# A gated linear-attention layer and an ELU feed-forward block: two engines' gating put in sequence, table loads placed by hand, and block sums moved

## The chip, the cores and the metric

The kernel runs on one core of a Trainium2 chip. The core has four compute engines that run their own instruction streams side by side and wait for one another through semaphores: TensorE (PE, matrix products), VectorE (DVE, elementwise work), ScalarE (ACT, functions by table, and copies) and GpSimd (POOL, elementwise work too). SyncE (SP) issues DMAs; GpSimd and ScalarE issue some as well. The metric is the device time of one execution in microseconds (us); lower is better. "Bank" below is a bank of PSUM, the memory that TensorE writes its sums to.

## The reference

The first block is a recurrence over 768 tokens, for 4 batches and 8 heads of 48 channels, with complex decay; only the real part is read out:

```python
mag = np.sqrt(a_re * a_re + a_im * a_im)
scale = np.minimum(mag, 0.999) / (mag + 1e-06)
a_re_n, a_im_n = (a_re * scale, a_im * scale)
for t in range(S):
    new_re = ar * S_re - ai * S_im
    new_im = ar * S_im + ai * S_re
    S_re, S_im = (new_re + kv, new_im)          # kv = outer product of k[t], v[t]
    y[:, :, t] = q[t] @ S_re
```

Its output, 3072 tokens by 384, goes through a feed-forward block: `h = x @ w_in` (384 by 2048), `g = ELU(h)`, `out = g @ w_out` (2048 by 384). All is float32.

## The kernel before

**Units.** A unit is two batches times 128 tokens; there are 12, numbered 0 to 11. Units u and u+2 hold the same batches, so state and the running angle pass from u to u+2. A unit goes through: the logarithm of the decay's magnitude and its angle (`squares`, `joined`, `logarithms`, `powers`, `lengths`, `ratios`, `slopes`, `angles`, `carried`: ACT, DVE, POOL), sums over tokens by TensorE (`decays`, `turns`), sine and cosine (`waves`, ACT), scaling of q and k by the decays (`scaled`), multiplication of q and k by sine and cosine (`gated`, line 1000), transposes (`transposed`, line 1020, copied out by ACT on line 1021), scores, states and values, and then the feed-forward layer of its 256 tokens.

**Gating.** `gated` is one multiplication of 128 by 1536 elements for k (tile `kg`) and one for q (tile `qg`). From unit 4 on, k's is done by GpSimd and q's by VectorE, issued k first. Both wait for the cosine (line 974).

**The angle's carry.** `carry_on` (line 859) sends the last token's angle of unit u by a DMA on GpSimd's queue to a row in device memory; `carry_back` (line 820) fetches that row by a second DMA on the same queue into one row of the tile `w`, once `slopes` (line 780) no longer reads it; `carried` (line 826) adds it to the angle of unit u+2, one instruction on VectorE; and `turns` (line 837, TensorE) sums the angles.

**The layer from unit 3 on.** The first product, by w_in, is done with 20 block products P0 to P19 (`mult`, line 1438, four blocks of 128 by 128 each) in place of 24. Their right-hand sides are the sums that `mixed` makes of the blocks of x (line 1406 on VectorE; line 1412, one sum, on GpSimd: it overwrites the block that the sum `pair` reads, so it waits for `pair`). Their left-hand sides are blocks of w_in and block sums of w_in (`summed_in`, lines 1394 and 1396), made once on VectorE. The 20 products add up in five banks (z, w, b, x, y) in the order `ORDER`; intermediate sums are taken out by ACT (`kept`, line 1451) and VectorE (`joint`, line 1454). A later product of the same bank therefore waits until the copy that needs the earlier sum is done: P3, the third product of bank z, waits for the copy of P8+P1 ("21"), and P12, the second of bank x, for the copy of P2 ("01"). The second product, by w_out, is done with seven (`product`, line 1316) in place of eight; its weight sums are made once by `combined` (line 1275), and its results leave by lines 1324, 1328, 1335, 1337 and 1341. The three banks b, z, w come free when these results have been read, w last of all (the third output sum of line 1337).

**ELU.** `low` (lines 1459 and 1460, ACT) makes exp(min(h,0)), `whole_of` (line 1463, VectorE) the rest. ACT holds one set of function tables at a time; where a function is not in the set that is loaded, the build puts a load (ACT_TABLE_LOAD) before the instruction.

**The order of the work** is written out by hand. Units 0 to 2 and part of unit 3 follow the list `first`, with idle products `warm` (line 1537) for TensorE between; what comes later is put at due times (`put`), in sixteenths of a unit's period, and sorted. Within one engine instructions run strictly in that order. Around the change, ACT has sine, absolute value, cosine, then the squares of the next unit, then the copies of the layer; TensorE has products of unit u's layer with the transposes of unit u+1 between; VectorE, in units 2 and 3, also makes the block sums of both weights, and from there tests weights (`test`, line 680).

Of the kernel before, what the change touches and what calls it, by code (L numbers as in the profile page):

```python
# [10 lines left out]
FP32 = mybir.dt.float32  # L11
U32 = mybir.dt.uint32
AF = mybir.ActivationFunctionType
ALU = mybir.AluOpType
PSUM = bass.MemoryType.PSUM

C = 128
# [488 lines left out]
def kernel(  # L506
# [12 lines left out]
    nc = tc.nc  # L519
# [4 lines left out]
    HD = H * D  # L524
# [161 lines left out]
    def flat(t):  # L686
        return t.rearrange("p n h d -> p (n h d)")
# [128 lines left out]

    def carry_back(u):

        if u in carry:
            nc.gpsimd.dma_start(out=flat(nat[u]["w"])[0:1], in_=carry[u])  # L820

    def carried(u):

        if u in carry:
            row = nat[u]["th"][0:1].rearrange("p n h d -> p (n h d)")
            nc.vector.scalar_tensor_tensor(
                out=row, in0=flat(nat[u]["w"])[0:1], scalar=float(2 * np.pi), in1=row, op0=ALU.mult,
                op1=ALU.add,
            )

# [24 lines left out]
    def carry_on(u):  # L855
        nxt = u + B // NB
        if nxt < NU:
            carry[nxt] = dram.tile([1, NB * HD], FP32, tag="carry", bufs=2, name="carry")
            nc.gpsimd.dma_start(out=carry[nxt], in_=flat(nat[u]["z"])[C - 1 : C])

    def turns(u):
# [126 lines left out]
            scaled(u, "k")  # L988
        nc.vector.tensor_tensor(out=x["q"], in0=x["q"], in1=x["E"], op=ALU.mult)

    def gated(u, part=None):

        x = nat[u]
        step = NB if part is None else 1
        n = part or 0
        for key in ("k", "q") if part is None else ("q", "k"):
            eng = products(u) if key == "k" else nc.vector
            each = x[key][:, n : n + step].rearrange("p n h d -> p (n h) d")
            to = gates[key][:, n : n + step].rearrange("p n h i d -> p (n h) i d")
            eng.tensor_tensor(  # L1000
                out=to[:, :, :, 0:D], in0=each.unsqueeze(2).to_broadcast([C, step * H, 2, D]),
                in1=x["cs"][:, n * H : (n + step) * H], op=ALU.mult,
            )
# [189 lines left out]
        inner(u, f)  # L1193
        elu(u, f)

    def table(name):
        nc.scalar.preload_act_table_set(name)

    def inner(u, f):
# [152 lines left out]
        "z": (8, 1, 3, 16, 17, 15), "w": (6, 5, 14, 10, 4, 11), "b": (7,), "x": (2, 12, 13),  # L1352
        "y": (9, 0, 18, 19),
    }
    ORDER = 8, 1, 7, 6, 3, 9, 5, 0, 2, 14, 12, 10, 16, 18, 4, 17, 19, 13, 11, 15
    IN_OF = {
# [41 lines left out]
    def mixed(u):  # L1398

        x = nat[u]  # L1400
        b = x["x"].rearrange("p k (n t) -> p (k n) t", n=2)
        six = new("x", 2, [C, NI, GT]).rearrange("p k (n t) -> p (k n) t", n=2)
        lo, hi = halves, pair

        def both(to, a, c, op):
            nc.vector.tensor_tensor(out=to, in0=a, in1=c, op=op)

        two = six[:, 0:1].to_broadcast([C, 2, C])
        both(six[:, 0:3], b[:, 0::2], b[:, 1::2], ALU.add)
        both(lo, b[:, 0:2], b[:, 2::3], ALU.add)  # L1410
        both(hi, two, six[:, 1:3], ALU.add)
        nc.gpsimd.tensor_tensor(out=six[:, 0], in0=b[:, 3], in1=b[:, 4], op=ALU.add)
        both(b[:, 2::3], b[:, 2:4], b[:, 4:6], ALU.subtract)
        both(six[:, 3:5], b[:, 0:2], six[:, 1:3], ALU.add)
        both(six[:, 5], lo[:, 0], lo[:, 1], ALU.add)
        x["mix"] = {
            0: hi[:, 1], 18: hi[:, 1], 15: hi[:, 0], 9: six[:, 1], 12: six[:, 1], 4: six[:, 2],
            2: six[:, 3], 10: six[:, 4], 16: six[:, 5], 5: six[:, 0], 17: lo[:, 0], 1: lo[:, 1],
            3: lo[:, 1], 19: b[:, 2], 7: b[:, 5], 6: b[:, 3], 8: b[:, 3], 11: b[:, 1],
            13: b[:, 0], 14: b[:, 4],  # L1420
        }

    def opened_banks(u):

# [124 lines left out]

    def decays_of(u, *at):  # L1550
        fns = squares, joined, logarithms, powers, lengths, ratios, slopes, noted, angles, carried
        put(at[6] + 0.3, carry_back, u)
        put(at[0], begun, u)
        for x, fn in zip(at, fns):
            put(x, fn, u)

    def gates_of(u, *at):
# [20 lines left out]
        (values, 0, 0), (powers, 1), (convert,), (states, 0, 1), (lengths, 1), (load_qk, 1),  # L1578
        (convert,), (ratios, 1), (values, 0, 1), (seam, 0), (warm, 2), (warm, 2), (decays, 1),
        (load_a, 2), (warm, 1), (inner, 0, 0), *2 * [(convert,)], (noted, 1), (scaled, 1),  # L1580
        (warm, 2), (convert,), (load_v, 1), (slopes, 1), (ends, 1), *3 * [(convert,)],
        (inner, 0, 2), (elu, 0, 0), (convert,), (fetch, "in", 4), (angles, 1), (turns, 1),
        (waves, 1), (gated, 1, 0), (inner, 0, 4), (gated, 1, 1), (transposed, 1, "q", 0),
        (transposed, 1, "k", 0), (convert,), (scores, 1, 0), (load_v, 2), (convert,),
# [13 lines left out]
        *3 * [(convert,)], (elu, 1, 12), (load_qk, 2), *4 * [(convert,)], (inner, 1, 14),  # L1598
        (elu, 1, 14), (logarithms, 2), (powers, 2), *4 * [(convert,)], (project, 1, 0, 0, 4),
        (project, 1, 1, 0, 4), *3 * [(convert,)], (noted, 2), (lengths, 2), (ratios, 2),  # L1600
        (slopes, 2), (carry_back, 2), (load_a, 3), (angles, 2), (carried, 2), (convert,), (project, 0, 1, 0, 4),
        (convert,), (project, 0, 0, 4, 8), *3 * [(convert,)], (decays, 2), (project, 1, 0, 4, 8),
        *2 * [(convert,)], (project, 1, 1, 4, 8), (turns, 2), *2 * [(convert,)],
        (project, 0, 1, 4, 8), (begun, 3), (squares, 3), *2 * [(convert,)],
# [1 line left out]
        (load_qk, 3), (logarithms, 3), (powers, 3), (project, 1, 1, 8, 12),  # L1606
        (states, 2, 0), (project, 1, 0, 12, 16), (transposed, 2, "q", 0), (lengths, 3),
        (ratios, 3), (project, 0, 0, 8, 12), (transposed, 2, "k", 0), (transposed, 2, "q", 1),
        (slopes, 3), (carry_back, 3), (angles, 3), (project, 1, 1, 12, 16), (transposed, 2, "k", 1),
        (carried, 3), (scored, 2), (turns, 3), (project, 0, 1, 8, 12), (valued, 2), (seam, 2),  # L1610
        (noted, 3), (project, 0, 0, 12, 16), (waves, 3), (scaled, 3), (ends, 3),
        (project, 0, 1, 12, 16), (opened,),
# [1 line left out]
    def layer_of(u, at_h, at_p):  # L1614
        if u == PAIRED:
            for m in range(NF // 2):
                put(at_h + m, hidden, u, 2 * m)
            put(at_h + 3, folded, u, 0, (3, 1))
            put(at_h + 7, folded, u, 1, (3, 1))
        else:  # L1620
            put(at_h, opened_banks, u)
            for n, p in enumerate(ORDER):
                put(at_h + 0.4 * n, mult, u, p)
            for at, fn, *args in (
                (1.5, kept, "21", "z"), (2.5, kept, "31", "b"),
                (3.5, joint, "31", "31", "w", ALU.add),
                (4.5, joint, "31", "31", "z", ALU.subtract), (5.6, low, "31", "31"),
                (6.6, whole_of, "31", "31"), (6.5, kept, "30", "w"),
                (7.5, joint, "20", "y", "21", ALU.subtract), (8.5, kept, "01", "x"),
                (9.5, kept, "10", "w"), (11.5, joint, "20", "20", "w", ALU.add),  # L1630
                (12.4, low, "20", "20"), (13.4, whole_of, "20", "20"),
                (12.5, joint, "30", "z", "30", ALU.subtract),
                (10.5, kept, "00", "x"),
                (13.5, joint, "00", "00", "y", ALU.add),
                (14.5, joint, "21", "21", "w", ALU.subtract), (15.4, low, "21", "21"),
                (16.45, whole_of, "21", "21"), (15.5, joint, "00", "z", "00", ALU.subtract),
                (16.4, low, "00", "00"), (17.45, whole_of, "00", "00"),
                (16.5, joint, "30", "30", "y", ALU.subtract), (17.4, low, "30", "30"),
                (18.45, whole_of, "30", "30"), (17.5, joint, "10", "x", "10", ALU.subtract),
                (18.4, low, "10", "10"), (19.55, whole_of, "10", "10"), (19.4, low, "11", "w"),  # L1640
                (20.4, whole_of, "11", "w"), (19.5, joint, "01", "01", "z", ALU.subtract),
                (20.5, low, "01", "01"), (21.5, whole_of, "01", "01"),
            ):
                put(at_h + 0.4 * at, fn, u, *args)
            put(at_h + 0.4 * 17.6, folded, u, 0, (3, 1))
            put(at_h + 0.4 * 22, folded, u, 1, (3, 1))
        ks = [(k, h) for k in (1, 4, 2, 5, 6, 7, 3) for h in range(2)]
        step = 8 / len(ks)
        for m, (k, h) in enumerate(ks):
            put(at_p + m * step, product, u, k, h)  # L1650
        for h in range(2):
            put(at_p + (2.2 + h) * step, folded, u, h, (2,))
            put(at_p + (6.2 + h) * step, folded, u, h, (4,))

    for u in range(2, NU):
# [4 lines left out]
        if u == 2:  # L1660
            decays_of(u, 16, 16, 17, 17, 18.4, 19.5, 19.6, 22.7, 19.8, 19.8)
            gates_of(u, 20.4, 21.6, 22.1, 22.4, 22.4, 22.6)
        else:
            sq = (r + 7.2, r + 9.6) if u == PAIRED + 2 else (r + 3.4, r + 5)
            decays_of(u, *sq, r + 12.8, r + 13.2, r + 13.4, r + 13.5, r + 14.9, r + 15.7, r + 15.5, r + 16.6)
            gates_of(u, r + 15, r + 18.32, r + 18.5, r + 18.6, r + 18, r + 19.7)
            if u > PAIRED + 1:
                put(r + 16.8, scaled, u, "k", None)
        if u > PAIRED:
# [5 lines left out]
            put(at, valued, u)  # L1675
            put(at, seam, u)
            put(r + 34.45, mixed, u)
        layer_of(u, r + 36, r + 44)
    for n in range(len(SUMS)):
        put(37 + 0.65 * n, summed_in, n)  # L1680
    for m, x in enumerate(((1, 0), (2, 0), (1, 1), (4, 0), (2, 1), (4, 1), (3, 0), (3, 1))):
        put(37.2 + m * 0.6, combined, *x)
    for m in range(NR):
        put(40 + 2.75 * m, test_fetch, m)
        put(42.2 + 2.75 * m, test)
# [41 lines left out]
```

## Time and profile before

| | us |
|---|---|
| median of 3 runs | 699.52 (698.95 to 702.98) |
| the profiled execution's own time | 702.24 |
| its span, first to last instruction | 700.4 |
| TensorE busy | 652.6 (93%) |
| VectorE busy | 519.8 (74%) |
| ScalarE busy | 426.6 (61%) |
| GpSimd busy | 172.9 (25%) |

A period of one unit in the steady part (units 4 to 11, from about 231 us on) takes about 53.2 us. TensorE's clock is full but for a few stretches. The views used are: the waits of TensorE (who was waited for, us in total, times, longest), the timeline (start, duration, engine, line, operation, tiles; in square brackets the idle time before it and who ended it), and a table of stretches (busy time of each engine, then the granted TensorE clock).

### The profile page before, as it was taken

What the parts mean: (1) busy time and instruction counts of PE and PEld (TensorE: products, weight loads), DVE (VectorE), ACT (ScalarE), POOL (GpSimd) and SP (SyncE); (2) the same over time, 40 slices, a digit from 0 to 9 for tenths busy, and PEclk for the clock granted to TensorE, in tenths of its full rate; (3) what the DMA queues carried; (4) which work ended last, traced back from release to release, by engine and by line L of the source; (5) the groups of instructions that cost most, each with busy time, mean ns of one, the idle gap of its engine ahead of it and who ended that gap; (6) DMA issues with size and microseconds to landing.
All of it is one profiled execution on the core that took longest, in us unless ns stands there. A gap on an engine that the chain in (4) does not pass through costs nothing.

```text
span 700.4 us, 17232 instructions
## 1 busy us (share of the span) xinstructions
PE 652.6 (93%) x7232; PEld 586.1 (84%) x7232; DVE 519.8 (74%) x790; ACT 426.6 (61%) x692; POOL 172.9 (25%) x202
## 2 busy tenths in 40 slices
PE   8899899899989899899899999999999899899995
PEld 6777686477878799899899899899899899899995
DVE  5889899763988868778678768868868858855381
ACT  6875356665726567577477477477477477372250
POOL 2000000122124404603603603703702701502000
PEclk9899999999989999999999999999999999999998
DMA  9996645330913521630652342441450560210000
GB/s 164 176 159 96 152 149 166 61 70 20 162 32 63 99 60 48 113 75 28 115 92 49 75 99 53 85 99 43 87 106 23 99 113 24 53 32 13 18 1 29
DMA packets 151507, 56.12 MB, mean 80 GB/s; under 512 B 129748, under 2 KB 143228, under 8 KB 151420
## 3 DMA queue, kind: packets, MB, share of 16 engines
q1 hardware_dynamic: 147616, 53.58, 38.0%
q0 software_dynamic: 3584, 1.21, 1.5%
q8 instruction: 59, 0.97, 0.6%
q14 instruction: 28, 0.23, 0.1%
q10 hardware_dynamic: 220, 0.14, 0.1%
HBM read 48.91 MB, written 4.81 MB: 77 GB/s over the span
## 4 chain that ended last, share of the span: by engine, by line
PE 45%; DVE 27%; ACT 19%; issue 6%; DMA 1%; ACTq 1%; POOL 0%; DVEq 0%; POOLq 0%
PE mlp L1316 16%; PE mlp L1438 6%; DVE qg L1000 5%; PE y L1438 5%; PE w L1020 4%; PE w L1061 3%; PE mlp L1207 3%; PE y L1106 3%; PE y L1133 2%; ACT L1460 1%; ACT L735 1%; ACT qt L1021 1%; DVE g L1454 1%; ACT ee L1460 1%; DVE n L842 1%
## 5 line engine op out<-in xcount | busy, mean ns | idle before, releaser
L1316 PE MATMUL mlp<-w_out,g 128*128 128x192 f32 x640 | 115.0, 331 | 3.0 <-DVE o L1337 2.8
L1316 PEld LDWEIGHTS mlp<-w_out,g 128*128 128x128 f32 x640 | 105.5, 192 | 7.1 <-DVE o L1337 5.1
L1078 POOL TENSOR_TENSOR S<-S,T 128x384 f32<-128x384 f32 x36 | 33.5, 930 | 204.4 <-DVE S L1076 204.4
L1207 PE MATMUL mlp<-x,w_in 128*128 128x256 f32 x288 | 68.2, 394 | 3.2 <-DVE g L1218 2.9
L1463 DVE SCALAR_TENSOR_TENSOR g<-ee,g 128x512 f32<-128x512 f32 x63 | 43.9, 696 | 31.9 <-ACT ee L1460 31.8
L1207 PEld LDWEIGHTS mlp<-x,w_in 128*128 128x128 f32 x288 | 55.8, 197 | 12.6 <-DVE g L1218 3.3
L1294 DVE TENSOR_TENSOR g<-g 128x512 f32<-128x512 f32 x80 | 59.2, 751 | 5.7 <-PE mlp L1316 4.6
L1438 PE MATMUL mlp<-x,w_in 128*128 128x128 f32 x432 | 58.5, 279 | 4.1 <-DVE o L1337 3.4
L1438 PEld LDWEIGHTS mlp<-x,w_in 128*128 128x128 f32 x432 | 52.4, 192 | 7.1 <-DVE o L1337 5.2
L1454 DVE TENSOR_TENSOR g<-g,mlp 128x512 f32<-128x512 f32 x45 | 30.7, 683 | 35.6 <-PE mlp L1438 34.8
L1316 PE MATMUL mlp<-w,g 128*128 128x192 f32 x320 | 54.7, 329 | 0.0
L1316 PEld LDWEIGHTS mlp<-w,g 128*128 128x128 f32 x320 | 51.8, 190 | 0.7
L1021 ACT COPY qt<-w 128x512 f32<-128x512 f32 x48 | 25.9, 589 | 43.5 <-PE w L1020 43.5
L1459 ACT ACTIVATE ee<-g 128x512 f32<-128x512 f32 x63 | 39.5, 627 | 19.3 <-DVE g L1454 18.9
L1460 ACT ACTIVATE ee<-ee 128x512 f32<-128x512 f32 x72 | 45.4, 631 | 2.1
L1187 POOL DMA_DIRECT2D x<-y x62 | 29.9, 489 | 59.6 <-ACT y L1123 37.1
L970 ACT ACTIVATE cs<-n 128x768 f32<-128x768 f32 (+1 forms) x14 | 10.5, 751 | 54.8 <-DVE n L845 54.8
L1000 DVE TENSOR_TENSOR qg<-q,cs 128x1536 f32<-128x1536 f32 (+1 forms) x12 | 40.4, 3367 | 0.0
L1020 PE MATMUL w<-ident,qg 128*128 128x128 f32 x192 | 26.6, 285 | 11.4 <-DVE qg L1000 11.2
L820 POOL DMA_DIRECT2D n<-carry x10 | 5.4, 538 | 121.9 <-DVE n L780 67.3
L1020 PEld LDWEIGHTS w<-ident,qg 128*128 128x128 f32 x192 | 22.7, 147 | 14.2 <-DVE qg L1000 13.7
L901 ACT ACTIVATE n<-w 64x384 f32<-64x384 f32 (+1 forms) x60 | 28.1, 486 | 9.3 <-PE w L886 8.7
(217 smaller groups left out, 1480.0 us busy)
## 6 DMA issues: line engine op xcount, KB each, us to landing
w<-in_moe_w_out_dram SPq DMA_DIRECT2D x8, 768.0 KB, 4.3
g<-in_moe_w_in_dram SPq DMA_DIRECT2D x24, 256.0 KB, 3.6
g<-in_moe_w_out_dram SPq DMA_DIRECT2D x24, 256.0 KB
w<-in_moe_w_in_dram SPq DMA_DIRECT2D x16, 288.0 KB, 5.4
vn<-in_v_dram SPq DMA_DIRECT2D x24, 192.0 KB, 4.2
out_dram<-o SPq DMA_DIRECT2D x48, 96.0 KB, 2.8
ar<-in_a_re_dram SPq DMA_DIRECT2D x22, 192.0 KB, 3.3
ai<-in_a_im_dram SPq DMA_DIRECT2D x22, 192.0 KB, 5.2
```

The lines of the kernel that those rows point to most:

```text
L1000: eng.tensor_tensor(out=to[:, :, :, 0:D], in0=each.unsqueeze(2).to_broadcast([C, step * H, 2, D]), in1=x["cs"][:, n * H : (n + step) * H], ...
L1020: nc.tensor.transpose(t[:, h], of, ident)
L1021: nc.scalar.copy(out=o[:, h0 : h0 + 4], in_=t)
L1078: eng.tensor_tensor(out=new_s, in0=new_s, in1=wide, op=ALU.mult)
L1207: nc.tensor.matmul(t[:, e], lhsT=w_in[:, i, ts(f + e, C)], rhs=x["x"][:, i], start=(i == 0), stop=(i == NI - 1),)
L1294: nc.vector.tensor_tensor(out=S_of(u, k, h), in0=a, in1=b, op=op)
L1316: nc.tensor.matmul(to, lhsT=a[:, m], rhs=b[:, m], start=(first and h == 0 and m == 0), stop=False, skip_group_check=True,)
L1438: nc.tensor.matmul(x["c" + c][:, ts(m, C)], lhsT=a[:, m], rhs=x["mix"][p], start=(p == BANKS[c][0] and m == 0), stop=False, skip_group_che ...
L1454: nc.vector.tensor_tensor(out=part(u, to), in0=part(u, a), in1=part(u, b), op=op)
L1459: nc.scalar.activation(out=e, in_=part(u, of), func=AF.Relu, scale=-1.0)
L1460: nc.scalar.activation(out=e, in_=e, func=AF.Exp, scale=-1.0)
L1463: nc.vector.scalar_tensor_tensor(out=part(u, to), in0=nat[u]["e", to], scalar=-1.0, in1=part(u, of), op0=ALU.add, op1=ALU.max,)
```

## The change

1. `gated` takes the tensors as an argument. For units 4 to 11, q's part (VectorE) is put at r+19.7 and k's (GpSimd) at r+19.8. Between them stands `mixed_rest`, which holds two operations taken out of `mixed`: VectorE's `pair` and GpSimd's sum that waits for it. GpSimd runs in order, so its gating of k now stands behind VectorE's gating of q. In unit 3 VectorE does q before k.
2. For units 4 to 11, one load of a table set that has arctangent and sine stands before `angles`, where two loads stood (one before the arctangent, one before the sine); and the load of the exponential's set stands behind the squares and ahead of the copies "21" and "31", where it stood between the two steps of the first `low`. That is one load fewer per unit.
3. P7 is the sixth product and not the third: 8, 1, 6, 3, 9, 7, 5, ... The sum "31" is made in another order accordingly: P6 is copied out of bank w, bank z subtracted, bank b added.
4. The block sums of w_in: the first 11 at steps of 0.6 and not 0.65, the other 10 (from 45.4 on) past unit 3's scores and states; the last two of `combined` at 46 and 47, where 40.8 and 41.4 were.
5. For units 2 and 3 the carried row stays on the chip, in a row of the tile `more`, so `carry_back` and its DMA are gone and `carried` reads that row.
6. One `warm` of 2 in the list `first` (ahead of unit 1's `ends`) is 4.

```diff
     def carry_back(u):
-        if u in carry:
+        if u in carry and u > 3:
             nc.gpsimd.dma_start(out=flat(nat[u]["w"])[0:1], in_=carry[u])
...
-                out=row, in0=flat(nat[u]["w"])[0:1], scalar=float(2 * np.pi), in1=row, op0=ALU.mult,
+                out=row, in0=carry[u] if u < 4 else flat(nat[u]["w"])[0:1], scalar=float(2 * np.pi), in1=row, op0=ALU.mult,
...
         if nxt < NU:
-            carry[nxt] = dram.tile([1, NB * HD], FP32, tag="carry", bufs=2, name="carry")
+            if nxt < 4:
+                carry[nxt] = more[0:1].rearrange("p a b -> p (a b)")[:, ts(nxt % 2, NB * HD)]
+            else:
+                carry[nxt] = dram.tile([1, NB * HD], FP32, tag="carry", bufs=2, name="carry")
             nc.gpsimd.dma_start(out=carry[nxt], in_=flat(nat[u]["z"])[C - 1 : C])
...
-    def gated(u, part=None):
+    def gated(u, part=None, keys=("k", "q")):
...
-        for key in ("k", "q") if part is None else ("q", "k"):
+        for key in keys if part is None else ("q", "k"):
...
-    ORDER = 8, 1, 7, 6, 3, 9, 5, 0, 2, 14, 12, 10, 16, 18, 4, 17, 19, 13, 11, 15
+    ORDER = 8, 1, 6, 3, 9, 7, 5, 0, 2, 14, 12, 10, 16, 18, 4, 17, 19, 13, 11, 15
...
-        two = six[:, 0:1].to_broadcast([C, 2, C])
         both(six[:, 0:3], b[:, 0::2], b[:, 1::2], ALU.add)
         both(lo, b[:, 0:2], b[:, 2::3], ALU.add)
-        both(hi, two, six[:, 1:3], ALU.add)
-        nc.gpsimd.tensor_tensor(out=six[:, 0], in0=b[:, 3], in1=b[:, 4], op=ALU.add)
...
+    def mixed_rest(u):
+        b = nat[u]["x"].rearrange("p k (n t) -> p (k n) t", n=2)
+        six = nat[u]["six"]
+        nc.vector.tensor_tensor(
+            out=pair, in0=six[:, 0:1].to_broadcast([C, 2, C]), in1=six[:, 1:3], op=ALU.add
+        )
+        nc.gpsimd.tensor_tensor(out=six[:, 0], in0=b[:, 3], in1=b[:, 4], op=ALU.add)
...
-        (warm, 2), (convert,), (load_v, 1), (slopes, 1), (ends, 1), *3 * [(convert,)],
+        (warm, 4), (convert,), (load_v, 1), (slopes, 1), (ends, 1), *3 * [(convert,)],
...
-                (1.5, kept, "21", "z"), (2.5, kept, "31", "b"),
-                (3.5, joint, "31", "31", "w", ALU.add),
-                (4.5, joint, "31", "31", "z", ALU.subtract), (5.6, low, "31", "31"),
-                (6.6, whole_of, "31", "31"), (6.5, kept, "30", "w"),
+                (1.5, kept, "21", "z"), (2.5, kept, "31", "w"),
+                (4.5, joint, "31", "31", "z", ALU.subtract),
+                (5.5, joint, "31", "31", "b", ALU.add), (6.6, low, "31", "31"),
+                (7.6, whole_of, "31", "31"), (6.5, kept, "30", "w"),
...
-            decays_of(u, *sq, r + 12.8, r + 13.2, r + 13.4, r + 13.5, r + 14.9, r + 15.7, r + 15.5, r + 16.6)
-            gates_of(u, r + 15, r + 18.32, r + 18.5, r + 18.6, r + 18, r + 19.7)
+            decays_of(u, *sq, r + 12.8, r + 13.2, r + 13.4, r + 13.5, r + 14.9, r + 15.7, r + 15.52, r + 16.6)
+            gates_of(u, r + 15, r + 18.32, r + 18.5, r + 18.6, r + 18)
+            put(r + 19.7, gated, u, None, ("q",))
+            put(r + 19.8, gated, u, None, ("k",))
+            if u > PAIRED + 1:
+                put(r + 19.45, table, "exp_and_others", u)
+                put(r + 15.5, table, "trig_and_small", u)
...
             put(r + 34.45, mixed, u)
+            put(r + 35.75, mixed_rest, u)
...
-        put(37 + 0.65 * n, summed_in, n)
+        put(37 + 0.6 * n if n < 11 else 45.4 + 0.6 * (n - 11), summed_in, n)
...
-        put(37.2 + m * 0.6, combined, *x)
+        put(37.2 + m * 0.6 if m < 6 else 40 + m, combined, *x)
```

More of the change, by code (lines that the diff above doesn't have):

```diff
@@ L1194, in hidden, with table @@
         elu(u, f)
-    def table(name):
+    def table(name, u=None):
         nc.scalar.preload_act_table_set(name)
@@ L1421, in mixed @@
         }
+        x["six"] = six
+    def mixed_rest(u):
[5 more added lines that the diff above has]
+        nc.gpsimd.tensor_tensor(out=six[:, 0], in0=b[:, 3], in1=b[:, 4], op=ALU.add)
     def opened_banks(u):
@@ L1551, in decays_of @@
         fns = squares, joined, logarithms, powers, lengths, ratios, slopes, noted, angles, carried
-        put(at[6] + 0.3, carry_back, u)
+        if u > 3:
+            put(at[6] + 0.3, carry_back, u)
         put(at[0], begun, u)
@@ L1600 @@
         (project, 1, 1, 0, 4), *3 * [(convert,)], (noted, 2), (lengths, 2), (ratios, 2),
-        (slopes, 2), (carry_back, 2), (load_a, 3), (angles, 2), (carried, 2), (convert,), (project, 0, 1, 0, 4),
+        (slopes, 2), (load_a, 3), (angles, 2), (carried, 2), (convert,), (project, 0, 1, 0, 4),
         (convert,), (project, 0, 0, 4, 8), *3 * [(convert,)], (decays, 2), (project, 1, 0, 4, 8),
@@ L1608 @@
         (ratios, 3), (project, 0, 0, 8, 12), (transposed, 2, "k", 0), (transposed, 2, "q", 1),
-        (slopes, 3), (carry_back, 3), (angles, 3), (project, 1, 1, 12, 16), (transposed, 2, "k", 1),
+        (slopes, 3), (angles, 3), (project, 1, 1, 12, 16), (transposed, 2, "k", 1),
         (carried, 3), (scored, 2), (turns, 3), (project, 0, 1, 8, 12), (valued, 2), (seam, 2),
```

## The prediction

> **What bounds the kernel now.** I read the waits of TensorE first, since it is busy for 93% of the span:
>
> ```profile
> PE w L1020 <- DVE qg L1000: 11.2, 8, 1.7
> PE mlp L1438 <- DVE o L1337: 3.4, 5, 1.7
> PE w L1061 <- DVE S L1076: 3.0, 3, 2.4
> PE w L837 <- DVE n L826: 2.7, 2, 1.6
> PE y L1438 <- ACT g L1451: 2.4, 8, 0.3
> ```
>
> The first and last rows come once in each of units 4 to 11; the third and fourth are single holes. The timeline of unit 7 shows the repeated one:
>
> ```profile
> 391.07 0.84 ACT L970 ACTIVATE cs<-n 128x768 f32<-128x768 f32 x1 [5.53 <-DVE n L845]
> ...
> 393.75 3.75 POOL L1000 TENSOR_TENSOR kg<-k,cs 128x1536 f32<-128x1536 f32 x1 [0.92 <-POOL x L1412]
> ...
> 394.26 0.82 ACT L710 ACTIVATE n<-ai 128x768 f32<-128x768 f32 x1
> 394.37 4.75 DVE L1000 TENSOR_TENSOR qg<-q,cs 128x1536 f32<-128x1536 f32 x1
> ...
> 394.99 1.05 ACT L1451 COPY g<-mlp 128x512 f32<-128x512 f32 x2
> ...
> 395.60 1.16 PE L1438 MATMUL mlp<-halves,g 128*128 128x128 f32 x8
> ...
> 399.17 1.09 PE L1020 MATMUL w<-ident,qg 128*128 128x128 f32 x8 [1.51 <-DVE qg L1000]
> ...
> 405.41 1.16 PE L1438 MATMUL y<-x,w_in 128*128 128x128 f32 x8 [0.30 <-ACT g L1451]
> ```
>
> q's gating takes 4.75 us beside GpSimd's; in unit 2, where VectorE does both, it takes 1.75. It ends 1.62 us after k's, so it stood still until then. P3 (395.60) starts when the copy "21" is out (394.99 to 395.52): just in time. The row at 405.41 is P12; after it TensorE runs without a hole to 430. So a unit's cost here is the time from the sine's start (391.07) to P12: 14.34 us in units 7 to 9, 14.31 or 14.32 in 5, 6, 10 and 11, 14.69 in 4.
>
> Last, the table of stretches about the hole in unit 3 (TensorE's busy time stands first, its clock third from the end):
>
> ```profile
> 200.00:202.00 2.00, 0.00 (x0) 0.00 (x0) 2.00 (x4) 0.00 (x0) 0.00 (x0) 0.98 0.03 10
> 202.00:204.00 2.00, 1.79 (x60) 1.78 (x60) 1.66 (x4) 0.00 (x0) 1.03 (x2) 0.50 0.03 8
> 206.00:208.00 2.00, 2.00 (x8) 2.00 (x7) 2.00 (x4) 0.94 (x2) 1.21 (x1) 0.50 0.00 0
> ```
>
> A hole of 2.41 us is followed by 6.6 us (202.0 to 208.6) at half clock.
>
> **Part 1, gating in sequence, with parts 2 and 3, for units 4 to 11.** They act on one stretch and are summed together, from unit 7's rows.
> VectorE: `pair` leaves the front (0.33), so the third output sum ends at 394.12 and not 394.45; q's gating runs 394.04 to 395.79, then `pair` to 396.12. Queued behind these on GpSimd: the sum of line 1412 (0.52), then k's gating 396.7 to 400.45, then line 716 and the state sums, which nobody needs before 420. Line 1454 reads one operand from PSUM and ran at its usual 0.73 beside GpSimd at 399.36, so VectorE's next work isn't held.
> ACT: the merged trigonometric load takes 1.28 us out of an idle stretch of 5.53: worth nothing; if that idle time were gone it would be worth 1.28. The exponential's load stands behind line 710 and ahead of the copies: 395.10 to 396.38, "21" to 396.93, "31" to 397.45.
> TensorE: P8, P1 from 391.60; P6 was covered by P7 and now needs bank w at once: it waits from 393.38 to 394.2 for line 1337. P3 needs "21": it waits from 395.1 to 396.97. Then nothing waits: P3, P9, P7 (3 of 0.893), q's transposes (0.873), P5, P0 (1.786), k's transposes (0.873, at 402.3; kg has been ready since 400.5), P2, P14 (1.786), and 0.1 for the restart: P12 at 405.06. ACT's copies "01" (to 404.95) are then only just in time. The sine-to-P12 time is 13.99, against 14.34.
> So of the removed wait of 1.51 nearly all comes back as P3's wait for the copy behind the load. Gain: 0.35 in units 5, 7, 8, 9, 10 (1.75), 0.7 in unit 4, 0 in unit 6 (there line 710 came a microsecond late for a DMA, which now delays P3), and 1.8 in unit 11, where no squares stand ahead of the load: 4.25 in all.
> The rule that speaks against it: the Trainium skill, "ScalarE: Activation LUTs", "What ACT_TABLE_LOAD costs", puts a switch of sets at about 2.66 us, 1.28 of load and 1.38 of drain. By that P3 would wait 1.3 us more in seven units: a loss of 5 rather than a gain of 4. But the row shows the Relu of line 1459 ending at 401.49, a load of 1.28, and the exponential starting at 402.80: 1.31 in all. I take the row.
>
> **The clock under the new holes.** TensorE now stands 0.8 us, works 0.9, and stands 1.9. The Trainium skill, "TensorE: Matmul & The Clock Gate", "HAM oscillation", asks only for no idle gap over about 3.4 us: by it nothing happens here. The rows disagree: the half clock came after 2.41 us. The stretches at half clock begin at 48.3, 79.0 and 202.0, whole multiples of some 3.41 us apart, so I read a window of 3.41 us. The one ended at 202.0 had 1.25 us of products (37%), that ended at 79.0 1.2 (35%); 1.7 (49%, 236.1 to 239.5) did not trip it. The new pattern leaves 0.9 us (26%) in a window that falls just right: between those thresholds 0.8 to 1.7 us of the 3.41 us of phases trip it, say 36%. Half clock for one window (as at 48.3) costs 1.7. In units 4 to 10 that is 7 x 0.36 x 1.7 = 4.3 us lost. Ends: 0 and 7 x 1.7 = 12.
>
> **Part 4, block sums.** Ahead of unit 3's first state sum two of line 1275 (0.9 each) and one of line 1394 (0.6) are gone from a VectorE that is full from 186 on: 2.4 us, so the hole of 2.41 closes, a wait of 0.24 at 194.89 too, and the half clock (6.6 us at half, 3.3 lost) with it. But they are put behind line 772 and ahead of line 826, on which unit 4's `turns` wait. There VectorE was full already (212.53 to 225.68):
>
> ```profile
> 222.57 2.31 POOL L979 TENSOR_TENSOR k<-k,n 128x768 f32<-128x768 f32 x1
> ...
> 223.13 2.55 DVE L826 SCALAR_TENSOR_TENSOR n<-n 1x768 f32<-1x768 f32 x1
> ```
>
> Line 772 to the end of 826 took 13.15 us; two of 1275 and one sum more make it 15.5 (line 979 still blocks about 1.7 us of it). In full clock TensorE reaches line 837 11.8 us after 772 starts, so it waits 3.7, where it waited 1.05. Carried through from 199.8 (products, line 1324, loads, logarithm, exponential at their rows): line 772 at 207.97 and not 212.53, line 837 at 223.5 and not 225.83. Gain 2.3 + 0.24. A hole of 3.7 trips the clock as surely as 2.41 did; about 1.0 of it is exposed, as the output sums of line 1337 hold TensorE there anyway. Net 1.5; ends: 5.9 (no new hole) and -0.8 (two windows fully exposed).
>
> **Part 5, the carry.** Unit 2's line 826 started at 129.28 for a DMA issued at 125.74; the angle was ready at 126.07. It now ends at 127.05 and line 837 starts when the products before it end, 128.63 for 130.28: 1.65. VectorE is then 3 us ahead; kg ends at 137.7 and TensorE comes at 137.93, so the 1.23 wait at 140.81 goes too: 2.9 (ends 1.65 and 2.9). Unit 3's carry wasn't waited for: 0. GpSimd's queue loses two issues of 0.54 us, with idle time about them; unit 3's order of q and k: 0 to 0.1.
>
> **Part 6.** Twelve products from 47.94 took 4.54 us at half clock, 2.75 at full. Two more idle products cost 0.6. If they hold the clock, 1.2 is gained; if not, 0.6 is lost. No row tells; I take 0.6 gained.
>
> **Sum.** 4.25 - 4.3 + 1.5 + 2.9 + 0.6 = 4.95 us. From the profiled execution's own 702.24: 697.3. The median of the runs is 2.7 lower: 694.5.
>
> **The rivals.**
> The clock holds in the steady units (26%): then 4.3 less, 690.2. For it: holes up to 1.74 us didn't trip it. Against: none of them had a second hole 0.9 us before.
> P3 is not held, because copies or load fall otherwise (7%): then the 1.5 and the 0.3 of eight units come free, about 13, with parts 4 to 6: 682. Against: the built order has the load ahead of both copies.
> The other side (12%): the clock gate in units 4 to 10, at the wait for "21". Two windows for each trip, as at 202, cost 3.4 us; in all seven units 23.8, and with the gains of 9.3 the time is 714; with one window in half of them it is 696. It decides from 9.3 / 1.7, so between five and six windows of half clock; with five trips of two windows it is 707.
> That the change doesn't do what it says: the built streams have GpSimd's gating behind `pair`, and loads fall from 5 to 4 a unit, so only the time is open.
>
> **Numbers.** The likeliest case (55%) is 694.5, from 690 to 699. Runs of before spread over 0.6%, so about 1% (7 us) is what can be told from no change. Faster by over 1% (below 692.5): most of the first two rivals and a fifth of the main case, 0.4; slower by over 1% (above 706.5): half of the third rival, 0.06; the rest 0.54. The range is 687 to 702: it leaves out the second rival and the worse half of the third.
>
> **What would show it.** q's gating at about 1.75 us with no wait at line 1020; a new wait of line 1438 for line 1451 of 1.9 us ahead of P3 in units 4 to 10, 13.5 us from P8 to P12; clock rows below 1.00 in two or three of these units; unit 3's wait at line 1061 gone and one of over 3 us at line 837; unit 2's line 826 right behind line 815. It is wrong if ACT's load or copies stand elsewhere, or if the clock falls in nearly every unit.

## The result and the profile after

| | before | changed |
|---|---|---|
| median of 20 runs each, us | 700.36 (697.71 to 702.98) | 702.14 (699.55 to 707.40) |
| ratio, 95% interval | | 1.0024 (1.0006 to 1.0041) |
| the profiled execution, us | 702.24 | 701.03 |
| its span, us | 700.4 | 699.3 |
| TensorE / VectorE / GpSimd busy, us | 652.6 / 519.8 / 172.9 | 651.5 / 498.9 / 156.5 |

The change is worth nothing: within 1%, and rather 0.24% slower. The forecast was 694.5 us. Lines of the changed kernel stand lower in the file: 1000, 1020, 1061, 1337, 1438 and 1451 of before are now 1003, 1023, 1064, 1340, 1449 and 1462.

The waits of TensorE in the changed kernel (who was waited for; us in total, times, longest):

```profile
PE mlp L1449 <- ACT g L1462: 17.9, 7, 3.8
PE w L837 <- DVE n L826: 3.5, 1, 3.5
PE mlp L1319 <- DVE o L1340: 2.8, 3, 1.1
...
PE w L1064 <- DVE S L1079: 1.4, 3, 0.8
...
PE w L1023 <- DVE qg L1003: 0.9, 1, 0.9
```

The wait for q's gating, 11.2 us in eight units, is down to 0.9 in one. In its place stands a wait for ScalarE's copy, 17.9 us in seven. Unit 8's timeline shows what stands ahead of that copy:

```profile
442.63 0.84 ACT L973 ACTIVATE cs<-n 128x768 f32<-128x768 f32 x1 [6.83 <-DVE n L845]
...
444.95 1.06 PE L1449 MATMUL mlp<-x,w_in 128*128 128x128 f32 x8
445.09 0.83 ACT L709 ACTIVATE n<-ar 128x768 f32<-128x768 f32 x1
445.18 0.35 DVE L1340 TENSOR_TENSOR o<-mlp,ee 128x192 f32<-128x192 f32 x1
445.45 1.75 DVE L1003 TENSOR_TENSOR qg<-q,cs 128x1536 f32<-128x1536 f32 x1
445.82 0.83 ACT L710 ACTIVATE n<-ai 128x768 f32<-128x768 f32 x1
446.66 1.28 ACT L1200 ACT_TABLE_LOAD   x1
...
447.96 1.07 ACT L1462 COPY g<-mlp 128x512 f32<-128x512 f32 x2
448.10 3.45 POOL L1003 TENSOR_TENSOR kg<-k,cs 128x1536 f32<-128x1536 f32 x1
...
448.60 1.16 PE L1449 MATMUL mlp<-halves,g 128*128 128x128 f32 x8 [2.59 <-ACT g L1462]
```

The row at 444.95 is P6; it starts before the third output sum of line 1340 does, so it doesn't wait for that. P3 (448.60) then waits in one piece, 2.59 us: behind the squares of the next unit (709, 710), the load, and the copy "21".

What that hole does is seen in the tables of stretches (TensorE's busy time first, its clock third from the end). Behind unit 7's hole (391.45 to 394.04), then in and behind unit 8's, which is of the same length:

```profile
395.00:397.00 2.00, 2.00 (x14) 2.00 (x14) 0.69 (x1) 0.00 (x0) 2.00 (x2) 0.63 0.14 52
397.00:399.00 2.00, 2.00 (x11) 2.00 (x11) 0.77 (x2) 0.00 (x0) 1.75 (x1) 0.51 0.00 0
...
448.00:450.00 2.00, 1.40 (x12) 1.41 (x13) 0.14 (x1) 1.03 (x2) 2.00 (x2) 1.00 0.39 122
450.00:452.00 2.00, 2.00 (x20) 2.00 (x20) 0.97 (x2) 0.00 (x0) 2.00 (x2) 1.00 0.03 9
```

In unit 7 TensorE ran at half clock for 3.4 us (395.54 to 398.95), in unit 8 not at all. Units 9 and 10 fell as unit 7 did; unit 6, with a hole of 3.79, fell for 6.8 us (337.51 to 344.33). The time from one unit's sine to the next one's shows the price (start times of line 970, now 973, from the timelines):

| from unit | 4 | 5 | 6 | 7 | 8 | 9 | 10 |
|---|---|---|---|---|---|---|---|
| before | 53.76 | 53.38 | 53.11 | 53.17 | 53.24 | 53.08 | 52.75 |
| changed | 53.09 | 53.07 | 56.83 | 54.56 | 52.82 | 54.35 | 54.06 |

So the profiled execution falls into three pieces. Up to unit 4's sine it is 5.74 us ahead (225.08 for 230.82). From there to unit 11's sine it loses 6.29 (378.78 for 372.49). Behind it, it gains 1.65. That makes 1.1 us ahead in all, where the median is 1.8 us behind: each trace is one execution, and these two are not the median ones.

### The profile page after: what moved, and what is told of

Same layout as the page of the kernel before. It is cut to its first block, busy times and chain, and to the rows that moved or that the text cites. A ratio compares the mean times of both kernels' runs of the same rounds, so it can differ in the third digit from the quotient of the medians.

```text
span 699.3 us, 17222 instructions
## 1 busy us (share of the span) xinstructions
PE 651.5 (93%) x7236; PEld 591.3 (85%) x7236; DVE 498.9 (71%) x790; ACT 418.9 (60%) x684; POOL 156.5 (22%) x200
## 4 chain that ended last, share of the span: by engine, by line
PE 58%; DVE 15%; ACT 14%; issue 4%; DMA 4%; SPq 4%; ACTq 0%; DVEq 0%
PE mlp L1319 13%; PE mlp L1449 11%; PE y L1449 8%; PE mlp L1210 6%; PE w L1023 5%; PE mlp L1235 3%; SPq L598 3%; PE y L1235 3%; PE w L1064 3%; PE y L1109 2%; DMA ai<-in_a_im_dram 2%; PE y L1136 2%; ACT L1200 2%; DVE g L1297 1%; ACT L735 1%
## 5 line engine op out<-in xcount | busy, mean ns | idle before, releaser
L1210 PE MATMUL mlp<-x,w_in 128*128 128x256 f32 x288 | 65.1, 381 | 3.2 <-DVE g L1221 2.3
L1474 DVE SCALAR_TENSOR_TENSOR g<-ee,g 128x512 f32<-128x512 f32 x63 | 43.8, 696 | 11.2 <-ACT ee L1471 11.1
L1471 ACT ACTIVATE ee<-ee 128x512 f32<-128x512 f32 x72 | 45.4, 631 | 2.3
L1449 PE MATMUL mlp<-halves,g 128*128 128x128 f32 x144 | 22.5, 305 | 17.9 <-ACT g L1462 17.9
L1449 PEld LDWEIGHTS mlp<-halves,g 128*128 128x128 f32 x144 | 19.8, 213 | 19.4 <-ACT g L1462 19.4
L1462 ACT COPY g<-mlp 128x512 f32<-128x512 f32 x36 | 20.4, 586 | 21.3 <-PE mlp L1449 21.2
L1449 PE MATMUL y<-x,w_in 128*128 128x128 f32 x216 | 31.9, 295 | 0.0
```

The lines of the kernel that those rows point to most:

```text
L1210: nc.tensor.matmul(t[:, e], lhsT=w_in[:, i, ts(f + e, C)], rhs=x["x"][:, i], start=(i == 0), stop=(i == NI - 1),)
L1449: nc.tensor.matmul(x["c" + c][:, ts(m, C)], lhsT=a[:, m], rhs=x["mix"][p], start=(p == BANKS[c][0] and m == 0), stop=False, skip_group_che ...
L1471: nc.scalar.activation(out=e, in_=e, func=AF.Exp, scale=-1.0)
L1474: nc.vector.scalar_tensor_tensor(out=part(u, to), in0=nat[u]["e", to], scalar=-1.0, in1=part(u, of), op0=ALU.add, op1=ALU.max,)
```

## The experiments

**The load behind the copies** (`late_load`).

```diff
-                put(r + 19.45, table, "exp_and_others", u)
+                put(r + 21.2, table, "exp_and_others", u)
```

> The changed kernel with one move: in units 4 to 11 the load of the exponential's tables stands behind the copies '21' and '31' and not ahead of them; everything else stays. Theory A (the load ahead of '21' makes one hole of some 2.6 us ahead of P3, and that hole trips TensorE's clock in about half of the units): P3 waits 1.28 us less in seven units, 9 us, and the half-clock stretches of units 6, 7, 9 and 10 go, 7 to 9 us: 684 to 687, ratio to before about 0.98. Rival B (the clock falls for the order of P7 and the clean cut of the two gatings, whatever the load does): only the 9 us come, about 693, ratio 0.99, half clock still in three or four units. Rival C (the load is not what P3 waits for; the squares ahead of it or VectorE are): no change, 702.

Measured: 682.56 us, ratio 0.9738 (0.9697 to 0.9778). One instruction moved behind two copies on its own engine is worth 2.9% against the changed kernel. Unit 8's rows, ScalarE's and TensorE's:

```profile
437.31 0.83 ACT L710 ACTIVATE n<-ai 128x768 f32<-128x768 f32 x1
438.04 1.05 ACT L1462 COPY g<-mlp 128x512 f32<-128x512 f32 x2
439.11 1.28 ACT L1200 ACT_TABLE_LOAD   x1
```

```profile
436.44 1.06 PE L1449 MATMUL mlp<-x,w_in 128*128 128x128 f32 x8
438.66 1.16 PE L1449 MATMUL mlp<-halves,g 128*128 128x128 f32 x8 [1.16 <-ACT g L1462]
```

The hole is 1.16 us instead of 2.59, and in units 5, 7, 8, 9 and 10 no clock falls. Only unit 6, whose line 710 comes 0.99 us late for a DMA, still has a hole of 2.27 and a window at half clock. That is theory A, and a little more than it asked for; B and C fall. What the merged load ahead of `angles` is worth by itself was not tried.

**The hole filled and not removed** (`fill`).

```diff
+            put(at_h + 1, idle, u, 8)          # behind P6, ahead of P3
...
+    def idle(u, n):
+        t = work([C, C])
+        for _ in range(n):
+            nc.tensor.matmul(t, lhsT=ident, rhs=ident, start=True, stop=True)
```

> The changed kernel with eight idle products (1.8 us at full clock) behind P6 and ahead of P3 in units 4 to 11; the load stays ahead of '21', so the wait for it stays, and only TensorE's idle time inside it is filled. Theory A (the holes cost twice, once as a wait and once through the clock): the half-clock stretches of units 6, 7, 9 and 10 go and the wait stays; 7 to 9 us less than the changed kernel, 693 to 695, ratio to before 0.990. Rival B (the clock falls for another reason, and late_load gained by the load's place alone): no gain, or a loss where the eight products outlast the hole: 702 to 704.

Measured: 696.54 us, ratio 0.9939 (0.9920 to 0.9958), 0.85% or 6 us below the changed kernel. Work that nobody needs makes the kernel faster. P3 comes no earlier for it:

```profile
438.96 1.95 PE L1555 MATMUL w<-ident 128*128 128x128 f32 x16
441.71 0.49 PE L1449 MATMUL mlp<-halves,g 128*128 128x128 f32 x2 [0.80 <-ACT g L1462]
```

The clock shows it in all the executions and not in the profiled one alone: over the whole span the granted clock was 0.961 to 0.976 in the 20 of the changed kernel (median 0.973) and 0.978 to 0.992 in the 18 of `fill` (median 0.986). In the trace of `fill`, from unit 5 on the clock is full until the end of the last layer, and the times from sine to sine are 52.4 to 53.4: those of unit 8 of the changed kernel (52.82), which had the hole and kept its clock. The two prices of the hole can now be told apart: some 6 us by the runs for the clock (8.4 in the two traces, over units 6, 7, 9 and 10), and the other 14 from `fill` to `late_load` for the wait itself and what follows from it, which is not taken apart further.

**Parts 1 to 3 alone, and parts 4 to 6 alone** (`p123`, `p456`; each is the changed kernel with the other three parts undone).

> Parts 1, 2 and 3 alone on the kernel before (gating in sequence, tables, P7 later), without the block sums, the carry and the two idle products. Theory A: the loss in units 4 to 11 stands alone here: 6 to 9 us slower than before, 706 to 709, ratio 1.009 to 1.013. Rival B (the three parts are harmless, and the late block sums of part 4 take the time): 4 us faster than before, 696, ratio 0.994.

> Parts 4, 5 and 6 alone on the kernel before (block sums, carry on the chip, two idle products). Theory A: what was gained up to unit 5, some 6 us, reaches the end: 694, ratio 0.991. Rival B (the sums behind line 772 cost what they gave, the trips of the clock included): 699 to 701, ratio 0.998 to 1.001.

Measured: `p123` 708.30 us, ratio 1.0108 (1.0074 to 1.0141); `p456` 698.73 us, ratio 0.9974 (0.9955 to 0.9994). The loss is in parts 1 to 3, as theory A says. Its TensorE waits begin with the same line as the changed kernel's:

```profile
PE mlp L1447 <- ACT g L1460: 20.3, 8, 3.5
```

But `p456` gave 1.8 us, not 6, and the two don't add up: +7.6 and -1.8 against +1.7 for all six parts together. A row of `p456` behind unit 4's sine says why:

```profile
227.29 3.91 DVE L1399 SCALAR_TENSOR_TENSOR w_in<-g,w_in 128x512 f32<-128x512 f32 x1
231.13 0.34 DVE L1340 TENSOR_TENSOR o<-mlp,ee 128x192 f32<-128x192 f32 x1
```

```profile
226.61 4.05 POOL L1003 TENSOR_TENSOR kg<-k,cs 128x1536 f32<-128x1536 f32 x1 [0.92 <-POOL x L1415]
```

```profile
231.53 0.79 PE L1452 MATMUL mlp<-x,w_in 128*128 128x128 f32 x2 [3.72 <-DVE o L1340]
```

The last of the moved sums, 0.69 us elsewhere, takes 3.91: with the gating in its old order it falls beside GpSimd's gating of k and ends with it. The output sum behind it is late, TensorE stands 3.72 us, and its clock falls (229 to 237). From unit 4's sine to unit 5's it takes 58.05 us where part 5 alone takes 53.75. In the changed kernel k's gating stands behind q's, and the same sum takes 0.69 (at 227.95). So part 1 shelters part 4.

**Parts 4, 5 and 6 one by one** (`only4`, `only5`, `only6`).

> Part 4 alone on the kernel before: the later sums of w_in behind unit 3's scores and states, the last two sums of w_out later. By the prediction's step 1.5 us faster, 699, ratio 0.998. Rival (the hole moves from unit 3's state to unit 4's line 837 and the clock falls there as well): no change or up to 2 us slower, ratio 1.000 to 1.003.

> Part 5 alone on the kernel before: the carried row of units 2 and 3 stays on the chip. By the prediction's step 2.9 us faster, 697.5, ratio 0.996. Rival (VectorE, full in units 2 and 3, takes it back at the next stretch that it bounds): 0 to 1 us, ratio 0.999 to 1.000.

> Part 6 alone on the kernel before: two more idle products ahead of unit 1's line 946. By the prediction's step 0.6 us faster, between 1.2 faster and 0.6 slower: ratio 0.9983 to 1.0009. If the early stretches at half clock move about from run to run whatever is done here: 1.000.

Measured: `only4` 702.02, ratio 1.0018 (0.9999 to 1.0037); `only5` 698.74, ratio 0.9974 (0.9955 to 0.9992); `only6` 700.45, ratio 1.0006 (0.9990 to 1.0023). Part 5 is a gain of 1.8 us (0.6 to 3.2). Part 6 can't be told from nothing. Part 4 alone is, if anything, a loss: line 837 waits 3.6 us and TensorE falls to half clock from 220 to 227 behind it, and the sum beside k's gating stalls here too (3.93 us, at 227.09).

**The table part left out** (`no_tables`: the changed kernel with its part 2 undone).

> The changed kernel without its part 2: the loads stand where the build puts them, the exponential's between the two steps of the first 'low', and there are five a unit again. Theory A (gating in sequence and P7 later carry the gain, the table part carries only the loss): near late_load, 683 to 686, ratio 0.977. Rival B (the loads by hand are worth something once they stand well: the one that is saved and the one taken out of the first 'low'): 688 or more, ratio above 0.982.

Measured: 691.70 us, ratio 0.9865 (0.9837 to 0.9893): rival B. Parts 1 and 3 to 6 gain 9 us without any load placed by hand; a well placed load gains 9 more. The waits show where most of those 9 are: with the load between the two steps of the first `low` again, P12 waits for the copy "01" behind it (second row; the first is P3's wait).

```profile
PE mlp L1449 <- ACT g L1462: 8.9, 7, 2.4
PE y L1449 <- ACT g L1462: 8.5, 8, 1.2
```

**The squares behind the copies too** (`late_squares`, on `late_load`; the load is put at r+21.3 and not r+21.2, still behind both copies).

```diff
-            sq = (r + 7.2, r + 9.6) if u == PAIRED + 2 else (r + 3.4, r + 5)
+            sq = (r + 7.2, r + 9.6) if u == PAIRED + 2 else (r + 5.1, r + 6)
```

> late_load with the next unit's squares (0.82 us each, and the sum of them on GpSimd) behind the copies '21' and '31' too, in units 5 to 11. Theory A (what is left of P3's wait, 1.2 us a unit, is for these squares): 1.2 us in six or seven units and no half clock at unit 6's layer, 673 to 675, ratio 0.961. Rival B (the copies of q's transposes, now queued behind squares and load, are late and hold TensorE instead): 680 to 683, ratio 0.971 to 0.974.

Measured: 679.68 us, ratio 0.9696 (0.9664 to 0.9727): between the two expectations. P3's wait is gone in every unit; half of what it had cost came back as another wait, of k's transposes for GpSimd, which was hidden under it:

```profile
PE w L1023 <- POOL kg L1003: 4.9, 8, 1.4
```

**Parts 1 and 3 taken out of the faster kernel** (`gate_old`: `late_squares` with part 1 undone; `p7_third`: `late_squares` with part 3 undone).

> late_squares with part 1 undone: k's gating issued first on GpSimd beside q's on VectorE, and the pair with its sum back ahead of them. If the two gatings hold each other up as in the kernel before: q's takes 4.7 us again, its transposes wait 1.5 us in eight units, 12 us more than late_squares, 691, ratio 0.987. If the wait was covered by the products that now come ahead: 680 to 683.

> late_squares with part 3 undone: P7 third again, as in the kernel before, and the sum '31' in its old order. The prediction's step (P7 later uncovers P6's wait for bank w, 0.8 us a unit): 5 to 6 us less, 674, ratio 0.962. Rival (P6 doesn't wait for bank w, as the changed kernel's trace shows, and the number of products ahead of q's transposes is the same): no change, 679 to 681, ratio 0.970.

Measured: `gate_old` 699.31 us, ratio 0.9975 (0.9952 to 0.9997); `p7_third` 679.48 us, ratio 0.9707 (0.9671 to 0.9744). P7's place is worth nothing. The gating in sequence is worth 20 us here, not 12:

```profile
444.88 4.75 DVE L1003 TENSOR_TENSOR qg<-q,cs 128x1536 f32<-128x1536 f32 x1
```

```profile
449.69 1.09 PE L1023 MATMUL w<-ident,qg 128*128 128x128 f32 x8 [2.00 <-DVE qg L1003]
```

```profile
452.00:454.00 2.00, 2.00 (x12) 2.00 (x11) 0.03 (x1) 1.71 (x3) 0.00 (x0) 0.50 0.10 33
```

q's gating takes 4.75 us as in the kernel before. But P3 no longer waits, so TensorE reaches q's transposes sooner, and the hole is 2.00 us where it was 1.51. At 1.51 the clock never fell; at 2.00 it fell in units 5, 7, 8 and 10 of 5 to 11.

**The hole at line 837** (`sums_gap`, on `late_squares`; `p456_gap`, the same on `p456`).

```diff
-        put(37 + 0.6 * n if n < 11 else 45.4 + 0.6 * (n - 11), summed_in, n)
+        put(37 + 0.6 * n if n < 11 else 45.39 if n < 15 else 45.4 + 0.6 * (n - 11), summed_in, n)
...
-... r + 14.9, r + 15.7, r + 15.52, ...
+... r + 14.9, r + (16.7 if u == PAIRED + 2 else 15.7), r + 15.52, ...
```

> late_squares with four of the moved sums of w_in ahead of line 772 (VectorE stood idle for 2.7 us there) and unit 4's two reductions of lines 796 and 799 behind line 826. If what part 4 lost is the work that it queued ahead of line 826: the wait of 3.5 us at line 837 goes, less 1.0 that the output sums of line 1340 hold anyway: 2.5 to 3.5 us less than late_squares, 676.5, ratio 0.965. If that hole is set by something else: no change, 679 to 680.

> p456 (parts 4, 5 and 6 on the kernel before) with four of the sums ahead of line 772 and unit 4's two reductions behind line 826, as in sums_gap. If part 4's gain was lost at line 837 alone: 3.5 us less than p456, 695, ratio 0.992. If the time saved up to unit 4 is taken back in units 4 and 5 in any case: 698 to 699, ratio 0.997.

Measured: `sums_gap` 676.22 us, ratio 0.9651 (0.9616 to 0.9685); `p456_gap` 697.28, ratio 0.9950 (0.9932 to 0.9967). The four sums fill a stretch in which VectorE had waited 2.69 us for ScalarE ahead of line 772, and unit 4's two reductions stand behind line 826:

```profile
216.55 1.53 PE L837 MATMUL w<-n,sum_turns 128*128 128x384 f32 x4 [0.18 <-DVE n L826]
220.91 2.87 PE L1319 MATMUL mlp<-w_out,g 128*128 128x192 f32 x16 [2.83 <-DVE o L1340]
```

The wait of 3.53 at line 837 is 0.18; 1.7 of it comes back as a longer wait for line 1340's sum, 2.83 where it was 1.11. From unit 3's sine to unit 4's it takes 54.83 us for 56.44, so 1.6 us are gained in the trace, and some 3 by the medians, whose intervals overlap. In `p456_gap` the sum that stalls beside k's gating remains, and with it a wait of 4.4 us for line 1340, so it gained less than the 3.5 us of the first expectation and, with 1.5 by the medians, somewhat more than the second.

**Two last ones** on `sums_gap`: k's first transposes behind P2 (`gap_kt`), and part 5 undone (`gap_no5`).

```diff
-                put(r + 23 + 2.3 * n, transposed, u, "k", n)
+                put(r + ((23.25 if u > PAIRED + 1 else 23), 25.3)[n], transposed, u, "k", n)
```

> sums_gap with k's first transposes one product later (behind P2) in units 4 to 11. They waited 0.6 us a unit for GpSimd's gating of k, which stands behind q's. If that wait is open time: 4 us less than sums_gap, 672.5, ratio 0.960. If the copy of P2 or of k's transposes on ScalarE is then late for P12 instead: no change, 676 to 677.

> sums_gap with part 5 undone: the row of units 2 and 3 goes through device memory again. By the prediction's step: 2.9 us more than sums_gap, 679, ratio 0.969. By what part 5 alone measured: 1.8 us more, 678, ratio 0.968. If a later stretch that VectorE bounds takes it back: no change, 676, ratio 0.965.

Measured: `gap_kt` 676.51 us, ratio 0.9657 (0.9618 to 0.9695), no change. The wait for k's gating falls from 5.1 to 1.0 us, and the one for the copy "01" takes its place:

```profile
PE y L1449 <- ACT g L1462: 2.8, 8, 0.6
```

`gap_no5`: 679.12 us, ratio 0.9714 (0.9681 to 0.9747). Part 5 is worth 2.9 us here by the medians, the step's figure, and 4.4 by the two ratios; their intervals leave it open between some 1 and 8, so the agreement proves little.

The fastest kernels are `sums_gap` and `gap_kt`: 3.5% below the kernel before, 3.7% below the changed one.

## Why the prediction was wrong

By the prediction's own steps:

1. **Parts 1 to 3, mechanism: right.** q's gating was forecast at about 1.75 us and is 1.75; the wait at line 1020 is gone; P3 waits for "21" behind the load, as forecast. In unit 8, where the clock held, sine to sine is 52.82 against 53.24, a gain of 0.42; the forecast was 0.35. Unit 11's 1.8 is 1.65 for the whole stretch behind its sine.
2. **P6's wait for bank w: wrong.** "it waits from 393.38 to 394.2 for line 1337": it doesn't wait. In the built stream, the first product into w carries no wait for VectorE when P6 comes third (changed kernel), and one when it comes fourth (`p7_third`). The banks seem to be given out in the order of their first use, so that moving P7 also moved the late bank; that is read from the stream and not shown by an experiment. The 0.8 us thus went to P3's wait: one hole of 2.59, not 0.8 and 1.9 with P6 between them.
3. **The clock, 4.3 us lost: the step that failed, by its size.** The prediction took a chance of 36% in seven units, one window each: 2.5 windows. The trace has five, one in each of units 7, 9 and 10 and two in unit 6. First, the 36% was summed wrongly. With its own pattern (0.8 idle, 0.9 of work, 1.87 idle), a window has under 1.25 us of work in 0.9 us of the 3.41 us of phases and under 1.7 us in 2.7, since the wait of 1.87 alone leaves 1.54 of work; it wrote 0.8 to 1.7. The middle is 52%, and the loss 6.2 us and not 4.3. Second, without P6 between them the two waits made one hole, and ten holes of 2.59 or 2.60 us (units 5 and 7 to 10 of the changed kernel and of `p123`) tripped the clock seven times. Third, unit 6's hole of 3.79 cost two windows. 2.45 of gain in units 4 to 10 less 4.3 would be a loss of 1.85 from unit 4's sine to unit 11's; the trace shows 6.29, so the clock and unit 6 together took 8.7. `fill` puts the clock at 6 us by the runs. What one trip costs (1.6 to 1.7 us, units 7, 9 and 10 against `fill`) was right.
4. **Unit 6 at nothing: wrong.** Its late line 710 (1.08 us behind a DMA) did not only use up the gain; it made the hole 3.79, with two windows at half clock behind it. Sine to sine it takes 56.83, 3.7 more than before, the largest single loss. In the kernel before the same line came 1.02 us late and no such hole followed.
5. **Part 4, 1.5 us: unsettled in size.** The hole at line 837 was forecast at 3.7 and is 3.5. The gain depends on whether the old hole of 2.4 us in unit 3 trips the clock in the run one looks at. From unit 3's sine to unit 4's, 58.90 in before and 58.25 in `only5`, where it did; 56.73 in `p123`, where it didn't; 56.43 in the changed kernel. So within the changed kernel the part gives between 0.3 and 2.5. Alone it was 1.4 us slower by the medians (0.1 faster to 2.6 slower), and its trace has a sum that stalls beside k's gating for 3.93 us, which the prediction did not see.
6. **Part 5, 2.9 us:** 1.8 alone (0.6 to 3.2), 2.9 in the faster kernel. **Part 6, 0.6 us:** not seen (0.7 faster to 1.6 slower).

In the trace the parts up to unit 4 gave 5.74 where 5.0 were forecast, and the end 1.65 for 1.8. The miss lies between: 4.4 us, the clock with unit 6. By the medians the forecast missed by 7.6 us. 0.8 of it is the median of before, which more runs put at 700.36 and not 699.52; what is left beyond the 4.4 can't be placed, since the front itself varies from one execution to the next: the six kernels that share it with the changed one reach unit 4's sine at 222.0 to 225.3 us, and before, `p123` and `only6`, without parts 4 and 5, at 226.5 to 230.9. The rival "P3 is not held", 682 us with 7%, comes near what the change would have been with its load two instructions later, 682.56; but P3 still waits 1.16 us there, so that the figures agree is in part luck.

Both rules that the prediction quoted from the Trainium skill, and set aside for the rows, failed here too. A switch of tables costs what the row said and not the 2.66 us quoted: the load starts at 446.66 and the copy behind it at 447.96, 1.30 us later. And keeping every idle gap under some 3.4 us doesn't protect the clock: 2.59 and 2.00 us were enough.

## What to carry to other kernels

A load of function tables took 1.28 us in every place that was tried, but only what is queued behind it on ScalarE pays for it; so ask of each candidate place what comes next on that engine and who waits for it, and put it behind the copies that TensorE waits for. Count a new hole of TensorE twice, as time and as a chance of half clock, and add it up with the holes beside it before deciding that it is short enough: here half clock came where some 1.9 us of idle time fell into one fixed window of 3.41 us. When a wait of TensorE goes, it reaches its next wait earlier: here each wait taken away after the load's (squares, line 837, k's gating) gave back half or all of it at the next one.

## What the runs showed of the hardware

**A threshold for the clock, with a phase.** Holes of TensorE from unit 4 on by length (from the timelines), and whether half clock followed:

| hole, us | where | fell |
|---|---|---|
| 1.16 or 1.17 | `late_load`, units 5 and 7 to 10 | 0 of 5 |
| 1.39 to 1.74 | before, units 4 to 11 | 0 of 8 |
| 2.00 or 2.01 | `gate_old`, units 5 to 11 | 4 of 7 |
| 2.27 to 2.78 | `late_load` and `no_tables`, unit 6; `gate_old` and `p123`, unit 4 | 4 of 4 |
| 2.59 or 2.60 | changed and `p123`, units 5 and 7 to 10 | 7 of 10 |
| 3.45 to 4.41 | `p123` and changed, unit 6; `p456` and `p456_gap`, unit 4 | 4 of 4 |

That equal holes fall or don't is a matter of where they lie. In each trace the starts of the stretches at half clock are whole multiples of 3.413 us apart (in the changed kernel 395.54, 501.35 and 555.96, for instance: 31 and 16 windows), to 0.01 us. So the clock is decided at the borders of fixed windows, and TensorE's busy time can be read for each window. These are the changed kernel's in units 7 and 8, with the same hole of 2.59 us:

```profile
392.13:395.54 3.41, 1.50 (x13) 1.50 (x14) 1.41 (x4) 2.33 (x3) 2.42 (x2) 1.00 0.24 78
446.74:450.15 3.41, 1.55 (x13) 1.55 (x14) 1.42 (x4) 2.28 (x3) 2.47 (x2) 1.00 0.25 78
```

The first has 1.91 us without a product, and half clock begins at its end; the second, whose border cuts the hole, has 1.86, and the clock stays. Counted so for the 3043 windows at full clock behind 60 us in the 17 traces kept:

| idle in the window, us | windows | half clock in the next |
|---|---|---|
| up to 1.85 | 2999 (122 of them over 1.0) | 0 |
| 1.86 to 1.90 | 8 | 2 |
| 1.91 and more | 36 | 36 |

So the threshold here is 1.9 us of idle time, 56% of a window. A lone hole of h us over 1.9 then falls in (h + 3.41 - 3.8) / 3.41 of the phases: 47% at 2.00 and 65% at 2.59, where 4 of 7 and 7 of 10 fell, and never up to 1.74. A border can even save a hole that is longer than a window: at line 837 of `late_squares` TensorE stands 3.53 us, which leaves 1.83 and 1.88 us of idle time in two windows, and the clock stays full. Ahead of 60 us the count doesn't hold: six windows with 0.3 to 1.1 us of idle time were followed by half clock. TensorE works on small products there (in before 32 of them, two columns wide, in 1.60 us at 45.73), which the profile counts as busy; why they fell was not tried.

The Trainium skill, "TensorE: Matmul & The Clock Gate", "The HAM clock gate (the 'warmup' mystery)", says that the window is 3413 ns and runs free of the kernel's start; the starts above agree with it. Its rule in "HAM oscillation" of 3.4 us of idle time doesn't agree with these rows.

**Two gatings on two engines don't add speed.** q's takes 4.75 us beside k's, with TensorE waiting behind it, and 1.75 alone; a sum of 0.69 us takes 3.91 in the same place. The Trainium skill, "SBUF — State Buffer", "Who interferes with whom", has it that a VectorE instruction with two inputs in SBUF contends with a GpSimd instruction that reads SBUF, and that the port they share is locked and not divided. These rows agree: q's ended 1.62 us after k's had, little under its 1.75 alone. The one at 3.91 shows that the instruction held up need not be the one that was meant.
